# Where the first curve, three buffers, two low parts and one piece of weight work stand in a retention and two-layer MLP kernel on Trainium2

## The chip, the cores and the metric

The kernel runs on one core of one Trainium2 chip. The metric is the time of one execution on the device, in microseconds (us); lower is better. Five engines take part, each with its own queue that it works through strictly in order: TensorE (PE; PEld is its weight load), VectorE (DVE), ScalarE (ACT), GpSimd (POOL) and SyncE (SP), which issues the DMAs.

## What is computed

A retention layer (attention with a state that decays by a factor per head) gives 1536 tokens of 512 numbers. Two feed-forward layers follow, the first with softplus, the second with a scaled, shifted square of relu:

```python
def _moe_ref(x, w_in, w_out):
    h = x @ w_in                                        # 1536x512 @ 512x2048
    g = np.maximum(h, 0.0) + np.log1p(np.exp(-np.abs(h)))
    return (g @ w_out).astype(np.float32)

def _moe2_ref(x, w_in, w_out, s, b):
    h = x @ w_in
    r = np.maximum(h, 0.0)
    g = s * (r * r) + b
    return (g @ w_out).astype(np.float32)
```

The weights are 64-bit floats in memory.

## The kernel before

**Numbers in two parts.** Every operand of a matmul is a high part (`xh`, `wh`, `gh`: the value rounded by a ScalarE copy, L112) and a low part (`xl`, `wl`, `gl`: value less high part, by GpSimd, L115). A product is three matmuls: high by high, high by low, low by high. `split(hi, lo, src, hi_eng, lo_eng)` does both steps. A weight half is loaded as `raw` (pairs of words) and made into `wm` by three VectorE steps (L290, L292, L300) with a ScalarE step (L295) between them; then it is split.

**Tiles and pairs.** The tokens are three tiles j = 0, 1, 2 of 512. The 16 blocks of the 2048 hidden numbers are taken in pairs, p = 0 to 7 for each layer `la`. For tiles 0 and 1 a pair is computed by `second(la, p)` as a 2x2 matrix product with seven instead of eight products (sums of weight blocks `ws`, split to `sh`, `sl`; sums of inputs `x1` to `x4`). Each product is a `six`: six matmuls of 128x512. The four results are c11, c12, c22 and c21 (first index the half of the pair, second the tile). Tile 2 follows as two blocks of twelve (`all_of`).

**Banks.** The sixes go to three PSUM banks, `h` (the code's `one`), `y` (`other`) and `third`. A bank is copied out by ScalarE (`kept`, L514, to the buffers `p1`, `p5`, `u2`) or added to by VectorE (`joined`, L566), and only then is overwritten.

**The curve of layer one.** `begin` takes relu of the sum (ScalarE, L580) to r; `middle` forms u = -2r + sum, which is -|sum|, on VectorE (L592) and applies softplus on ScalarE (L593); `finish` adds r and u on GpSimd (L604) and puts the piece on the list `late_parts`; the next `end_part` takes it from there to `parts_g` (high part on ScalarE, low part on GpSimd). Where the sum still lies in a PSUM bank, L592 is the last that reads the bank. For c21 the sum is in bank `h`, and r and u go to named buffers (`tags`), before the change `u2` and `p1`.

**Second matmul.** `accs[k]` are twelve matmuls each (L630, or L403 for the blocks of the first stage) that multiply an earlier piece g by the second weights into four banks `acc`; each second such group is followed by the removal of `acc` into `xa` (additions on VectorE, L640; at the end of the first stage plain ScalarE copies, L410). The next group into `acc` waits for them.

**What sets the order.** The code is written in the order of issue for every engine; nothing is rearranged. `part`, `go_first`, `end_part` and `go_last` step generators that make the next weights: `go_first` issues two steps (L290, then L292 and L295), `end_part` the split of the weights before, `go_last` the third step.

**The place.** P0 = 2: `second(0, 2)` is the first pair computed this way, right after the retention stage and after `third_first`. It returns before tile 2, which `third_first` has done. There `accs` are: nothing, the last group of the first stage (with four L410 copies), and the two groups of tile 2. The pair after it, `second(0, 3)`, begins with a six into `h`, and its `accs[0]` and `accs[1]` use c11 and c21 of the pair before. The other touched place is `second(1, 2)` (`before`: the last pair before layer two also halves tile 2).

Of the kernel before, what the change touches and what calls it, by code (L numbers as in the profile page):

```python
# [41 lines left out]
P0 = FG // 2  # L42
# [6 lines left out]
def tile_retention_mlps(ctx: ExitStack, tc: tile.TileContext, head, w1, w2, sb, out):  # L49
    nc = tc.nc  # L50
# [560 lines left out]
    late_parts = []  # L611

    def parts_g(la, p, half, j, c):
        gg_t[la, p, half, j] = gh, gl = next_g()
        split(gh, gl, c, nc.scalar, nc.gpsimd)

    def acc_2(la, p, j, half, banks=FIRST + SECOND):
        wh, wl = w_t[la * NF + 2 * p + half, 1]
# [156 lines left out]
    with tc.manual_schedule():  # L775
# [135 lines left out]
        def part(to):  # L911

            nonlocal late_work, work
            late_work, work = work, split_next(to)
# [107 lines left out]
        def second(la, p, accs=None):  # L1022

            w = la * NF + 2 * p
            base = at[la, p + 1]
            halved = la and p >= HALVED
            final = not la and p == PAIRS - 1
            base -= halved
            (ah, al), (bh, bl), (sh, sl) = w_t[w, 0], w_t[w + 1, 0], s_t[w]
            a11, a12 = (ah[:, :KH], al[:, :KH]), (ah[:, KH:], al[:, KH:])  # L1030
            a22 = bh[:, KH:], bl[:, KH:]
            s1, s2, s3, s4 = ((sh[:, k], sl[:, k]) for k in range(4))
            b11, b21 = ((xh[0][:, k : k + 2], xl[0][:, k : k + 2]) for k in (0, 2))
            b22 = xh[1][:, 2:4], xl[1][:, 2:4]
            t1, t2, t3 = (x_t[k] for k in (1, 2, 3))

            of_tiles = (0, 1) if not la and p == P0 + 1 else (1, 2)
            accs = accs or [prior(la, p - 1, j, half) for j in of_tiles for half in range(2)]
            one, other, third = bank(ps_h, "h"), bank(ps_y, "y"), bank_2[1]

            before = la and p == HALVED - 1
            held = la and p == 1
            part(base + 2)
            six(one, a11, b11, True)
            p1 = kept(one, "p1")
            six(third, a12, b21, True)
            c11 = begin(la, joined(third, p1, not la), own=bool(la))
            end_part()
            go_first(bool(la))
            middle(c11)  # L1050
            accs[0]()
            if not held:
                finish(la, p, 0, 0, c11)
            go_last()
            if before:
                z = sum_z(3)
                next(z)

            part((base + 3) * (la or p != P0 + 1))
            six(other, s1, t1, True)  # L1060
            p5 = kept(other, "p5")
            six(one, s2, t2, False)
            u2 = kept(one, "u2")
            if held:
                finish(la, p, 0, 0, c11)
            end_part()
            go_first(bool(la))
            if before and not held:
                go(z, 2)
            accs[1]()  # L1070
            go_last()

            if final:
                part(base + 4)
                six(one, s3, t3, False)
                c22 = begin(la, joined(one, p5), own=True)
                end_part()
                go_first()
                middle(c22)
                accs[2]()  # L1080
                six(one, a22, x_t[4], False)
                c21 = begin(la, one, tags=("p5", "p1"))
                finish(la, p, 1, 1, c22)
                go_last()
                middle(c21)
                finish(la, p, 1, 0, c21)

                part(base + 5)
                six(other, s4, b22, False)
                c12 = begin(la, joined(other, u2, True))  # L1090
                end_part()
                go_first()
                middle(c12)
                accs[3]()
                finish(la, p, 0, 1, c12)
                go_last()
            else:
                part(base + 4)
                six(other, s4, b22, False)
                c12 = begin(la, joined(other, u2, not la), own=bool(la))  # L1100
                six(one, s3, t3, False)
                c22 = begin(la, joined(one, p5), own=True)
                if before:
                    if held:
                        go(z, 2)
                    else:
                        go(sum_z(1), 3)
                end_part()
                go_first(bool(la))
                middle(c12)  # L1110
                middle(c22)
                accs[2]()
                finish(la, p, 0, 1, c12)
                finish(la, p, 1, 1, c22)
                go_last()
                if before:
                    parts_z(3)

                part(base + 5)
                six(one, a22, x_t[4], False)  # L1120
                c21 = begin(la, one, tags=("u2", "p1"))
                if before and held:
                    go(sum_z(1), 3)
                end_part()
                go_first(bool(la))
                if not la and p == P0:
                    middle(c21)
                    accs[3]()
                else:
                    accs[3]()  # L1130
                    middle(c21)
                finish(la, p, 1, 0, c21)
                go_last()
                if before:
                    parts_z(1)

            if not la and p == P0:
                return
            if halved:
                last_tile(la, p, base, third, (a11, a12, a22), (s1, s2, s3, s4))  # L1140
                return
            part(base + 6)
            all_of(third, (ah, al), 2)
            ha = begin(la, third)
            end_part()
            go_first(bool(la))
            if before:
                go(sum_z(2), 2)
                go(sum_z(4), 2)
            middle(ha)  # L1150
            whole(*of_pair(la, p, 0, 0))
            finish(la, p, 0, 2, ha)
            go_last()
            if before:
                parts_z(2)
            if final:
                whole(*of_pair(la, p, 0, 1))
                x_whole(0)

            part(base + 7)  # L1160
            other = bank(ps_y, "y")
            all_of(other, (bh, bl), 2)
            hb = begin(la, other)
            end_part()
            go_first(bool(la))
            middle(hb)
            whole(*of_pair(la, p, *((1, 0) if final else (0, 1))))
            finish(la, p, 1, 2, hb)
            go_last()
            if final:  # L1170
                whole(*of_pair(la, p, 1, 1))
                x_whole(1)
                go(split_next(at[1, 1] + 1), 3)
            if before:
                parts_z(4)
# [171 lines left out]
```

## Time and profile before

| | us |
|---|---|
| median of 3 runs (563.3 to 563.73) | 563.42 |
| the profiled execution, its own time | 563.28 |
| its span, first to last instruction | 561.5 |
| TensorE busy in the span | 554.2 (99%) |
| VectorE / ScalarE / GpSimd busy | 388.4 / 362.6 / 384.4 |
| TensorE's waits that the profile names: 1.4 at the start, 1.2 on a copy L514, 0.9 on a low part L115, 0.2 on a high part L112 | 3.7 |

The span is what lies between the first and the last instruction; 1.8 us of the execution lie around it. A matmul's duration in the trace covers its way through the array, so neighbours overlap: in a dense row one starts every 0.227 us and lasts 0.39. The clock that was granted to TensorE was 1.00 of full speed over the whole span.

### The profile page before, as it was taken

The page shows a single profiled execution, that of the slowest core. Times are in us where ns is not written, and L with a number is a line of the kernel's source. Part 1 is how long each engine was busy: PE and PEld are TensorE (multiplying, and loading weights), DVE is VectorE, ACT ScalarE, POOL GpSimd, SP SyncE. Part 2 cuts the span into 40 slices and gives each one's busy share as a digit, 9 for nine tenths or more (in the row PEclk, how much of TensorE's full clock was granted, in tenths as well). Part 3 has the DMA queues.
Part 4 walks back from the last instruction along what each step waited for, and adds up shares of the span by engine and source line. Part 5 has one row for each costly group of instructions (what it writes and reads, how often), then busy time and mean ns, then how long its engine had stood idle before and what let it go on. Part 6 is the DMA issues. An engine that isn't in the chain of part 4 may idle for free.

```text
span 561.5 us, 8354 instructions
## 1 busy us (share of the span) xinstructions
PE 554.2 (99%) x3044; PEld 460.9 (82%) x3044; DVE 388.4 (69%) x588; ACT 362.6 (65%) x661; POOL 384.4 (68%) x323
## 2 busy tenths in 40 slices
PE   8999999999999999999999999999999999999997
PEld 7877888887688888888888887888788888888886
DVE  4887767776566958575789997598855655656334
ACT  4766662557456556555567888769497786868561
POOL 4457469879779796969797796749666655646230
PEclk9999999999999999999999999999999999999999
DMA  8996111211221312131231222221321121110005
GB/s 342 405 362 223 41 39 37 76 38 42 72 76 37 111 38 77 39 100 51 76 110 41 75 75 76 75 76 37 114 72 49 69 75 49 64 40 0 1 12 214
DMA packets 15017, 50.62 MB, mean 90 GB/s; under 512 B 1792, under 2 KB 2048, under 8 KB 14976
## 3 DMA queue, kind: packets, MB, share of 16 engines
q1 hardware_dynamic: 14976, 50.08, 25.6%
q8 instruction: 24, 0.39, 0.3%
q14 instruction: 17, 0.14, 0.1%
HBM read 46.93 MB, written 3.15 MB: 89 GB/s over the span
## 4 chain that ended last, share of the span: by engine, by line
PE 93%; DVE 3%; POOL 1%; ACT 1%; DMA 1%; issue 0%; POOLq 0%; DVEq 0%
PE acc L630 40%; PE h L500 12%; PE y L500 9%; PE acc L403 5%; PE h L352 5%; PE third L500 5%; PE y L508 4%; PE third L508 4%; PE y L191 2%; PE s L172 2%; PE h L191 1%; DVE p L551 1%; PE h L508 1%; PE y L352 1%; POOL gl L115 1%; PE acc L172 1%
## 5 line engine op out<-in xcount | busy, mean ns | idle before, releaser
L115 POOL TENSOR_TENSOR gl<-c,gh 128x512 fp32r<-128x512 f32 x78 | 103.2, 1331 | 65.0 <-ACT gh L112 45.3
L640 DVE TENSOR_TENSOR xa<-acc,xa 128x512 f32<-128x512 f32 x151 | 94.4, 683 | 76.0 <-PE acc L630 76.0
L115 POOL TENSOR_TENSOR wl<-wm,wh 128x512 fp32r<-128x512 f32 x64 | 86.7, 1355 | 77.9 <-ACT wh L112 77.8
L630 PE MATMUL acc<-wh,gh 128*128 128x512 f32 x190 | 74.3, 391 | 0.1
L630 PE MATMUL acc<-wh,gl 128*128 128x512 f32 x190 | 74.2, 391 | 0.0
L112 ACT ACTIVATE gh<-c 128x512 fp32r<-128x512 f32 x78 | 49.3, 631 | 13.1 <-POOL c L604 9.5
L630 PE MATMUL acc<-gl,wh 128*128 128x512 f32 x144 | 56.1, 390 | 0.9 <-POOL gl L115 0.9
L630 PE MATMUL acc<-gh,wh 128*128 128x512 f32 x144 | 56.3, 391 | 0.3 <-ACT gh L112 0.2
L630 PE MATMUL acc<-wl,gh 128*128 128x512 f32 x190 | 53.2, 389 | 0.0
L300 DVE SCALAR_TENSOR_TENSOR wm<-wm,cu,word 128x512 uint32<-128x512 uint32 x54 | 39.9, 739 | 4.2 <-ACT wm L295 3.5
L295 ACT ACTIVATE wm<-raw 128x512 f32<-128x512 f32 x64 | 42.4, 663 | 0.1
L292 DVE SCALAR_TENSOR_TENSOR word<-raw,cu,word 128x512 uint32<-128x512 uint32 x54 | 40.8, 756 | 1.9
L112 ACT ACTIVATE wh<-wm 128x512 fp32r<-128x512 f32 x64 | 39.7, 620 | 3.7 <-DVE wm L300 3.6
L630 PEld LDWEIGHTS acc<-wh,gh 128*128 128x128 f32 x190 | 35.8, 188 | 7.5 <-DVE xa L640 0.5
L630 PEld LDWEIGHTS acc<-wl,gh 128*128 128x128 f32 x190 | 35.7, 188 | 7.5
L630 PEld LDWEIGHTS acc<-wh,gl 128*128 128x128 f32 x190 | 35.8, 188 | 6.8
L599 ACT ACTIVATE c<-c,sbt 128x512 f32<-128x512 f32 x48 | 39.2, 816 | 1.6
L604 POOL TENSOR_TENSOR c<-c 128x512 f32<-128x512 f32 x28 | 36.8, 1323 | 4.3 <-ACT c L593 4.3
L630 PE MATMUL acc<-gh,wl 128*128 128x512 f32 x144 | 38.5, 389 | 0.0
L290 DVE TENSOR_SCALAR word<-raw 128x512 uint32<-128x512 uint32 x54 | 37.0, 686 | 0.5
L573 ACT ACTIVATE c<-c 128x512 f32<-128x512 f32 x21 | 13.1, 633 | 35.2 <-DVE c L566 35.2
L115 POOL TENSOR_TENSOR sl<-ws,sh 128x512 fp32r<-128x512 f32 x26 | 35.1, 1372 | 0.0
(277 smaller groups left out, 1406.7 us busy)
## 6 DMA issues: line engine op xcount, KB each, us to landing
raw<-w SPq DMA_DIRECT2D x64, 512.0 KB, 3.6
qk<-head SPq DMA_DIRECT2D x12, 512.0 KB, 8.3
kv<-head SPq DMA_DIRECT2D x12, 512.0 KB, 8.5
out<-xa SPq DMA_DIRECT2D x11, 256.0 KB, 2.1
cst<-head SPq DMA_DIRECT2D x1, 518.0 KB, 4.5
cst<-head SPq DMA_DIRECT2D x1, 256.0 KB, 5.5
out<-xa SPq DMA_DIRECT2D x2, 128.0 KB, 1.8
sbt<-sb SPq DMA_DIRECT2D x1, 1.0 KB, 10.3
```

The source lines that it names most:

```text
L112: nc.scalar.activation(hi, src, AF.Copy)
L115: lo_eng.tensor_tensor(out=lo, in0=src, in1=hi.bitcast(F32), op=ALU.subtract)
L290: nc.vector.tensor_scalar(out=x, in0=lw, scalar1=29, scalar2=None, op0=ALU.logical_shift_right)
L292: nc.vector.scalar_tensor_tensor(out=x, in0=hw, scalar=cu[:, 0:1], in1=x, op0=ALU.bitwise_and, op1=ALU.bitwise_or)
L295: nc.scalar.activation(m, hw.bitcast(F32), AF.Copy, scale=REBIAS)
L300: nc.vector.scalar_tensor_tensor(out=m.bitcast(U32), in0=m.bitcast(U32), scalar=cu[:, 1:2], in1=x, op0=ALU.logical_shift_left, op1=ALU.bit ...
L500: nc.tensor.matmul(ps, w[a][:, k * P : (k + 1) * P], x[b][:, k], start=start and i == 0, stop=i == len(ops) - 1, skip_group_check=True,)
L508: nc.tensor.matmul(ps, w[a][:, k * P : (k + 1) * P], (xh, xl)[b][j][:, k], start=i == 0, stop=i == len(ops) - 1)
L599: nc.scalar.activation(c, c, AF.Identity, scale=sbt[:, 0:1], bias=sbt[:, 1:2])
L604: nc.gpsimd.tensor_tensor(out=c, in0=c, in1=u, op=ALU.add)
L630: nc.tensor.matmul(acc_t[la, p, "pair", j][cc], *ops[i], start=half == 0 and i == 0, stop=half == 1 and i == 2)
L640: nc.vector.tensor_tensor(out=dst, in0=ps, in1=dst, op=ALU.add)
```

## The change

In `second(0, P0)`, named `first` below: the first curve (c11) is no longer begun right behind `joined`, but after the copies `p5` and `u2`; its `finish` and its high and low part come behind `accs[1]`. The curve of c21 uses the buffers `u2` and `p5`. The low parts of c12 and c22 go to VectorE. In `second(1, 2)` the step `go_first` of the last piece stands behind the group and its additions.

```diff
     def parts_g(la, p, half, j, c):
-        split(gh, gl, c, nc.scalar, nc.gpsimd)
+        split(gh, gl, c, nc.scalar, nc.vector if not la and p == P0 and j == 1 else nc.gpsimd)
...
+            first = not la and p == P0
...
-            c11 = begin(la, joined(third, p1, not la), own=bool(la))
+            c11 = joined(third, p1, not la)
+            if not first:
+                c11 = begin(la, c11, own=bool(la))
             end_part()
             go_first(bool(la))
-            middle(c11)
+            if not first:
+                middle(c11)
             accs[0]()
-            if not held:
+            if not (held or first):
                 finish(la, p, 0, 0, c11)
             go_last()
...
             u2 = kept(one, "u2")
+            if first:
+                c11 = begin(la, c11)
+                middle(c11)
...
             accs[1]()
+            if first:
+                finish(la, p, 0, 0, c11)
+                parts_g(*late_parts.pop())
             go_last()
...
-                c21 = begin(la, one, tags=("u2", "p1"))
+                c21 = begin(la, one, tags=("u2", "p5" if first else "p1"))
...
             end_part()
-            go_first(bool(la))
+            if not before:
+                go_first(bool(la))
             middle(hb)
             whole(*of_pair(la, p, *((1, 0) if final else (0, 1))))
+            if before:
+                go_first()
             finish(la, p, 1, 2, hb)
```

ScalarE's queue at the start of `second(0, 2)`: `c_1468` (after the change `c_1495`) is the relu of c11, L593 its softplus, `p5` and `u2` the copies, `wh0` high parts of weights, `gh` of c11, `xa2<-acc` the removal. Before:

```order
L514 ACTIVATE p1_1459<-h_1451 128x512
L580 ACTIVATE c_1468<-third_1171 128x512
L112 ACTIVATE wh0_1442<-wm_1444 128x512
L295 ACTIVATE wm_1475<-raw_1239 128x512
L593 ACTIVATE c_1470<-c_1470 128x512
L514 ACTIVATE p5_1491<-y_1452 128x512
L514 ACTIVATE u2_1499<-h_1451 128x512
L112 ACTIVATE gh_1501<-c_1468 128x512
L112 ACTIVATE wh0_1473<-wm_1475 128x512
L410 ACTIVATE xa2_111<-acc01_1332 128x512 x2
```

The same stretch of ScalarE's queue with the change:

```order
L514 ACTIVATE p1_1459<-h_1451 128x512
L112 ACTIVATE wh0_1442<-wm_1444 128x512
L295 ACTIVATE wm_1472<-raw_1239 128x512
L514 ACTIVATE p5_1485<-y_1452 128x512
L514 ACTIVATE u2_1493<-h_1451 128x512
L580 ACTIVATE c_1495<-third_1171 128x512
L593 ACTIVATE c_1497<-c_1497 128x512
L112 ACTIVATE wh0_1470<-wm_1472 128x512
L410 ACTIVATE xa2_111<-acc01_1332 128x512 x2
L410 ACTIVATE xa2_111<-acc2_1333 128x512
L410 ACTIVATE xa2_111<-acc3_1334 128x512
L112 ACTIVATE gh_1519<-c_1495 128x512
```

The two curve steps moved behind the two copies, the high part of c11 behind the removal, and the second weights' high part behind the softplus.

GpSimd's queue from the first weights' low part (`wl0`) to c22's sum (`c_1546`); the row `c_1468<-c_1468,c_1470` is c11's sum. Before:

```order
L115 TENSOR_TENSOR wl0_1443<-wm_1444,wh0_1442 128x512
L604 TENSOR_TENSOR c_1468<-c_1468,c_1470 128x512
L115 TENSOR_TENSOR gl_1502<-c_1468,gh_1501 128x512
L115 TENSOR_TENSOR wl0_1474<-wm_1475,wh0_1473 128x512
L319 TENSOR_TENSOR ws_1523<-wm_1475 128x256
L319 TENSOR_TENSOR ws_1523<-ws_1523,wm_1444 128x256
L319 TENSOR_TENSOR ws_1523<-wm_1444,wm_1475 128x256
L319 TENSOR_TENSOR ws_1523<-wm_1444,ws_1523 128x256
L604 TENSOR_TENSOR c_1535<-c_1535,c_1537 128x512
L604 TENSOR_TENSOR c_1546<-c_1546,c_1544 128x512
```

GpSimd's queue over the same work with the change:

```order
L115 TENSOR_TENSOR wl0_1443<-wm_1444,wh0_1442 128x512
L115 TENSOR_TENSOR wl0_1471<-wm_1472,wh0_1470 128x512
L604 TENSOR_TENSOR c_1495<-c_1495,c_1497 128x512
L115 TENSOR_TENSOR gl_1520<-c_1495,gh_1519 128x512
L319 TENSOR_TENSOR ws_1523<-wm_1472 128x256
L319 TENSOR_TENSOR ws_1523<-ws_1523,wm_1444 128x256
L319 TENSOR_TENSOR ws_1523<-wm_1444,wm_1472 128x256
L319 TENSOR_TENSOR ws_1523<-wm_1444,ws_1523 128x256
L604 TENSOR_TENSOR c_1535<-c_1535,c_1537 128x512
L604 TENSOR_TENSOR c_1546<-c_1546,c_1544 128x512
```

The second weights' low part now stands ahead of c11's sum and low part; the four sums of weights and the sums of c12 and c22 keep their places behind them.

VectorE's queue at the end of `second(0, 2)`, from the curves of c12 (`c_1537`) and c22 (`c_1544`) to that of c21, which reads bank `h_1451`. Before:

```order
L592 SCALAR_TENSOR_TENSOR c_1537<-c_1535,y_1452 128x512
L592 SCALAR_TENSOR_TENSOR c_1544<-c_1546,c_1544 128x512
L290 TENSOR_SCALAR word_1170<-raw_1287 128x512
L292 SCALAR_TENSOR_TENSOR word_1170<-raw_1287,cu_99,word_1170 128x512
L592 SCALAR_TENSOR_TENSOR p1_1582<-u2_1581,h_1451 128x512
L640 TENSOR_TENSOR xa2_111<-acc01_1552,xa2_111 128x512 x2
```

VectorE's queue there with the change:

```order
L592 SCALAR_TENSOR_TENSOR c_1537<-c_1535,y_1452 128x512
L592 SCALAR_TENSOR_TENSOR c_1544<-c_1546,c_1544 128x512
L115 TENSOR_TENSOR gl_1585<-c_1535,gh_1584 128x512
L115 TENSOR_TENSOR gl_1589<-c_1546,gh_1588 128x512
L290 TENSOR_SCALAR word_1170<-raw_1287 128x512
L292 SCALAR_TENSOR_TENSOR word_1170<-raw_1287,cu_99,word_1170 128x512
L592 SCALAR_TENSOR_TENSOR p5_1582<-u2_1581,h_1451 128x512
L640 TENSOR_TENSOR xa2_111<-acc01_1552,xa2_111 128x512 x2
```

The two low parts entered the queue ahead of the weight words and of the curve step of c21; on GpSimd they stood behind the two `sl`.

## Rows read from the trace of the kernel before

**Rows 1.** Waits of TensorE: who waited for whom, total, times, longest

```profile
PE y L500 <- ACT p L514: 1.2, 1, 1.2
```

**Rows 2.** TensorE in order of time, 125 to 151: start, us, what [idle before]

```profile
125.72 1.07 PE L403 MATMUL acc<-gh,wl 128*128 128x512 f32 x4
...
127.96 0.50 PE L500 MATMUL y<-xh,sh 128*128 128x512 f32 x1 [1.17 <-ACT p L514]
...
131.05 0.50 PE L630 MATMUL acc<-gh,wh 128*128 128x512 f32 x1
...
137.99 0.39 PE L500 MATMUL h<-xh,wh 128*128 128x512 f32 x1
...
146.85 0.50 PE L630 MATMUL acc<-gh,wh 128*128 128x512 f32 x1 [0.23 <-ACT gh L112]
148.27 0.50 PE L630 MATMUL acc<-gl,wh 128*128 128x512 f32 x1 [0.93 <-POOL gl L115]
...
150.90 0.39 PE L500 MATMUL y<-xh,sh 128*128 128x512 f32 x1
```

**Rows 3.** ScalarE in order of time, 124 to 139

```profile
126.79 0.63 ACT L593 ACTIVATE c<-c 128x512 f32<-128x512 f32 x1 [0.24 <-DVE c L592]
127.33 0.58 ACT L514 ACTIVATE p<-y 128x512 f32<-128x512 f32 x1
...
129.94 2.03 ACT L410 ACTIVATE xa<-acc 128x512 f32<-128x512 f32 x4
...
136.09 0.58 ACT L580 ACTIVATE u<-h 128x512 f32<-128x512 f32 x1
...
138.06 0.63 ACT L112 ACTIVATE gh<-c 128x512 fp32r<-128x512 f32 x1 [0.62 <-POOL c L604]
```

**Rows 4.** VectorE in order of time, 119 to 138

```profile
120.14 1.79 DVE L492 TENSOR_TENSOR x4l<-u,x4h 128x512 fp32r<-128x512 f32 x1
...
123.43 0.75 DVE L300 SCALAR_TENSOR_TENSOR wm<-wm,cu,word 128x512 uint32<-128x512 uint32 x1
...
134.13 0.68 DVE L290 TENSOR_SCALAR word<-raw 128x512 uint32<-128x512 uint32 x1
134.85 0.76 DVE L292 SCALAR_TENSOR_TENSOR word<-raw,cu,word 128x512 uint32<-128x512 uint32 x1
136.70 0.69 DVE L592 SCALAR_TENSOR_TENSOR p<-u,h 128x512 f32<-128x512 f32 x1 [1.10 <-ACT u L580]
```

**Rows 5.** GpSimd in order of time, 129 to 145

```profile
129.59 1.30 POOL L115 TENSOR_TENSOR gl<-c,gh 128x512 fp32r<-128x512 f32 x1 [0.74 <-ACT gh L112]
...
132.09 0.75 POOL L319 TENSOR_TENSOR ws<-wm 128x256 f32<-128x256 f32 x1
...
135.47 2.56 POOL L604 TENSOR_TENSOR c<-c 128x512 f32<-128x512 f32 x2
...
143.00 1.29 POOL L604 TENSOR_TENSOR u<-u,p 128x512 f32<-128x512 f32 x1
```

**Rows 6.** TensorE in order of time, 394 to 396 (layer two)

```profile
394.47 0.61 PE L500 MATMUL third<-xh,wl 128*128 128x512 f32 x2
395.14 0.50 PE L630 MATMUL acc<-wh,gh 128*128 128x512 f32 x1
```

**Rows 7.** VectorE in order of time, 392 to 397 (layer two)

```profile
392.42 0.68 DVE L290 TENSOR_SCALAR word<-raw 128x512 uint32<-128x512 uint32 x1
...
393.80 2.48 DVE L640 TENSOR_TENSOR xa<-acc,xa 128x512 f32<-128x512 f32 x4
```

**Rows 8.** Busy us by stretch: PE, PEld, DVE, ACT, POOL, granted clock, DMA share, GB/s

```profile
558.00:559.00 1.00, 0.47 (x4) 0.26 (x3) 0.64 (x2) 0.00 (x0) 0.00 (x0) 1.00 1.04 381
...
562.00:563.00 1.00, 0.00 (x0) 0.00 (x0) 0.00 (x0) 0.00 (x0) 0.00 (x0) 0.82 0.00 0
```

**Rows 9.** TensorE in order of time, 4 to 10: scores of one shape

```profile
4.48 1.23 PE L172 MATMUL s<-qk 64*128 64x128 f32 x8
...
8.88 0.71 PE L172 MATMUL s<-qk 64*128 64x128 f32 x8
```

More of the change, by code (lines that the diff above doesn't have):

```diff
@@ L1125, in second @@
                 go_first(bool(la))
-                if not la and p == P0:
+                if first:
                     middle(c21)
@@ L1135, in second @@
                     parts_z(1)
-            if not la and p == P0:
+            if first:
                 return
```

## The prediction

> **What bounds the kernel now.** I read the page's busy times first: TensorE works 99% of the span, so time can come or go only where TensorE waits, and every other engine counts only through that. Then the waits of TensorE: besides the start, the longest single one stands on a copy into `p5` [rows 1]. Then TensorE's order of time from 125 to 151 us, where that wait and the other two lie [rows 2]; a dense row there starts a matmul every 0.227 us (the last four of a group take 1.07, three steps and one duration of 0.39), and after a wait the next two starts lie about 0.13 further apart than that. Last the queues of ScalarE, VectorE and GpSimd over the same stretch [rows 3 to 5], since each piece of layer one passes through all three.
>
> Three gaps can be read. The group that starts its last four at 125.72 leaves TensorE free at 125.72 + 4 x 0.227 = 126.63, and the six into `y` starts at 127.96: 1.33 lost, because the copy of `y` (127.33 to 127.91) queued behind a softplus [rows 3]. From 137.99 to 150.90 stand 48 matmuls, 48 x 0.227 = 10.9 of 12.9 us: 2.0 lost, nearly all at 146.85 and 148.27, where TensorE waits for the high and the low part of c21, whose sum GpSimd only forms at 143.00 [rows 5]. In layer two, 394.47 + 2 x 0.227 = 394.92, and the next group starts at 395.14 [rows 6]: 0.22 and the slower start, 0.35.
>
> **Part one, the first curve behind the copies.** On ScalarE a pass follows another at about 0.52. The weights' `wm` is ready at 123.43 + 0.75 = 124.18 [rows 4], so without the curve ahead of them the queue runs: high part 124.2, L295 124.7, copy `p5` 125.3 to 125.9, copy `u2` 125.8, relu 126.2 to 126.8. TensorE finds the copy done and starts into `y` at 126.63, without a gap. Then VectorE's curve step 126.9 to 127.6, softplus 127.6 to 128.2, the second weights' high part 128.1, and the removal of the first stage's sums from 128.65 instead of 129.94. Its first two copies free the bank pair after half of 2.03 [rows 3], at 129.7. TensorE asks for that bank at 126.63 + 12 x 0.227 = 129.35 and waits 0.4, as it waited before. It starts at 129.75 instead of 131.05 [rows 2]. Gain so far 1.3; TensorE would then ask for bank `h` for the next pair at 129.75 + (137.99 - 131.05) = 136.7.
>
> **What that does to GpSimd.** The second weights' low part now stands ahead of c11's sum, and its high part comes from ScalarE only at 128.7. So: `wl` 128.8, sum of c11 130.05 to 131.35, high part on ScalarE 131.4 (behind the removal, which ends at 130.7), low part 132.1. Before, that low part ran at 129.59 and a weight part still followed it. From the first `ws` to the sums of c12 and c22 the queue took 135.47 - 132.09 = 3.4 [rows 5]. With 1.25 for the low part, `ws` now begins at 133.35 and the sums at 136.7, so that of c22 ends at 139.3, instead of 138.0. No work is added here; it comes 1.25 later.
>
> **Part two, two low parts on VectorE.** This is the term that decides. VectorE's queue is strict, and the two low parts now stand ahead of L290, L292 and c21's curve step L592, the last reader of bank `h`. Before, that step ran at 136.70, right behind its relu at 136.09 [rows 3, 4], and the next pair's six into `h` started at 137.99 without a wait. Now the second low part needs c22's high part: ScalarE 139.3 to 139.95 (before at 138.06). It starts at 140.0 at the earliest. How long it takes there is not shown: 0.69 is a VectorE pass alone, 1.79 one that subtracts two SBUF tiles while GpSimd works [rows 4], and here GpSimd works on (`sl`, right behind the sums). Behind it stand 0.68 + 0.76 + 0.69 = 2.1 [rows 4]. With 0.69 bank `h` comes free at 142.8; with 1.79 for both low parts (138.75, 140.55, 142.35) at 144.4. I take 143.9, since the row with 1.79 is the same operation on the same kinds of tiles. The Trainium skill, GPSIMD Engine Reference, section Specifications, says that GpSimd shares its SBUF interfaces with VectorE and contends with VectorE instructions that have two SBUF inputs; the 1.79 agrees, and by it the later end is the right one.
>
> So the next pair starts at 143.9 instead of 137.99: 5.9 later (4.8 to 6.4). TensorE stands idle from about 136.9 to 143.9, 7 us, where before it never waited over 1.4.
>
> **What the stall hides.** The three steps left of c21 (softplus 143.9, GpSimd's sum 144.6 to 145.9, then high and low part behind the next pair's copy and relu, about 150.2) are ready before TensorE asks for them, at 143.9 + 0.13 + 36 x 0.227 = 152.2. So the 2.0 of gaps after 137.99 go, but for the 0.13 of the restart: 1.9 back. GpSimd's relief of two passes and the free buffer `p1` (the next pair's copy no longer waits for the sum in `u2` and `p1`) would have been worth just that 1.9; they buy nothing more here. Net of the pair: 5.9 - 1.9 = +4.0 (2.9 to 4.5).
>
> **Part three, layer two.** The four additions L640 start at 393.80 behind L290 and L292, which began at 392.42 [rows 7]. Moved ahead, they start 1.4 earlier, the bank pair is free near 393.8, and TensorE goes on at 394.92: -0.35. The two weight steps end where the additions ended before, so L300 behind them, and with it the next weights, keep their time. ScalarE's L295 keeps its place in its own queue, and so does the load that SP issues with it.
>
> **The clock.** Before, TensorE's granted clock stayed at the upper of its two levels, 2.4 GHz, with no wait over 1.4 us. It falls once, behind the end: its last matmuls lie in the second 558 to 559 (0.47 us of it busy), and the second 562 to 563 has a mean of 0.82, so it fell to the lower level, 1.2 GHz, about 4 us after the last matmul [rows 8]. An idle time of 7 us is longer than that, so I expect it to fall in the stall. At the lower level half of the time is lost. For how long, no row shows directly; nearest is the kernel's start, where eight score matmuls took 1.23 at 4.48 and the same eight 0.71 at 8.88 [rows 9], although the page notes the full clock for both. TensorE began there at 1.45, so slow work lasted between 4.3 and 7.4 us, worth 2.1 to 3.7. I take 2.3, near the lower end, as matmuls stand denser behind the stall. The bound below is 0. The Trainium skill, TensorE: Matmul & The Clock Gate, section "HAM oscillation — how this bites in real kernels", says that a TensorE that waits long between two bursts of matmuls begins the next burst at the lower clock; it speaks against this change, and the one fall in the trace agrees.
>
> **The sum**, against the profiled execution's 563.28 (0.14 below the median of 563.42, which I leave aside): +4.0 for the pair, -0.35 for layer two, +2.3 for the clock, about +5.9: 569.2.
>
> **The rivals.**
> - *The stall without the clock.* TensorE's stall is shorter than 7, or the clock falls late or not at all: 563.28 + 4.0 - 0.35 = 566.9, with the bounds of the stall 565.8 to 567.5. For it speaks that nothing in the kernel shows a wait between 1.4 and 4 us; against it the fall behind the end. 0.25.
> - *The change does what its places suggest, and nothing is held.* This asks that c22's high part is there before c21's relu, so that VectorE's two low parts fit into its idle time before 136.70. Then the gaps go: 1.3 + 1.9 + 0.35 = 3.6 less, 559.7. It decides at the end of c22's sum on GpSimd: it must come by about 135, and even before it ended at 138.0 behind the same sums [rows 5]. 0.04.
> - *The hold is small.* If GpSimd gets to the sums some 3 us earlier than I work out, the stall is about 3 us and cancels with the gains: 562.2 to 564.4 (within 0.2%). It would take the weights' low part off the wait for ScalarE, and the queue rows show no such way. 0.04.
> - *A larger loss*, from a clock that stays down longer, 571 and more. 0.07.
>
> **How the numbers follow.** Forecast 0.60 (568.2 to 570.8). The range runs from 566.0, which takes in most of the case without the clock, to 571.0; outside it lie the faster and the even case, the lowest part of the first rival and the larger loss, about 0.2. Faster by over 0.2% (1.1 us, about what a measurement of this kernel can tell from no change) 0.04, within it 0.04, slower 0.92.
>
> **What would show it.** Right: in the new trace the six into `y` near 126.6 without a wait; TensorE idle for some 6 to 7 us ahead of the six into `h` of the next pair, released by L592 on VectorE, and ahead of that two L115 on VectorE, the second waiting for ScalarE's `gh`; no wait at the group that uses c21; a granted clock below 1.00 right behind the stall and matmuls twice as far apart there; no gap at the group in layer two. Wrong: L592 of c21 within a microsecond of its relu, or a six into `h` that starts ahead of it. If the stall is there and the clock stays at 1.00, the first rival holds and only the 2.3 falls.

## The result, and the profile after the change

The changed kernel takes 569.15 us (median of 4 runs, 568.42 to 569.39), the kernel before 563.44 on the same chip (4 runs, 563.30 to 563.73). The ratio is 1.0098, 95% interval 1.0081 to 1.0116: slower by 5.7 us, about 1%. The profiled execution of after took 568.42, with a span of 566.6 and a mean granted clock of 0.997; the rows below come from it. It is the fastest of the four runs: one of the others had the same mean clock (568.98), two had 0.994 (569.32 and 569.39).

The page's busy times of after (us, share of the span, instructions):

```profile
PE 555.2 (98%) x3044; PEld 462.4 (82%) x3044; DVE 390.6 (69%) x590; ACT 363.0 (64%) x661; POOL 382.9 (68%) x321
```

The waits of TensorE in the touched pair, after (who waited for whom, total, times, longest):

```profile
PE h L500 <- DVE p L592: 5.0, 1, 5.0
PE h L500 <- DVE c L566: 1.4, 1, 1.4
PE acc L630 <- ACT xa L410: 0.3, 1, 0.3
```

The shares of busy time hardly moved. What moved is in the waits: the one on the copy into `p5` [rows 1] is gone and so are those of c21's group [rows 2]; a wait of 5.0 us on L592 and one of 1.4 on L566 have come. TensorE in order of time, after (start, us, what, idle time before and who ended it):

```profile
126.90 0.39 PE L500 MATMUL y<-xh,sh 128*128 128x512 f32 x1
...
130.12 0.50 PE L630 MATMUL acc<-gh,wh 128*128 128x512 f32 x1 [0.34 <-ACT xa L410]
...
134.50 0.50 PE L500 MATMUL h<-x4h,wh 128*128 128x512 f32 x1 [1.37 <-DVE c L566]
...
143.88 0.79 PE L500 MATMUL h<-xh,wh 128*128 128x512 f32 x1 [5.00 <-DVE p L592]
144.47 0.63 PE L500 MATMUL h<-xl,wh 128*128 128x512 f32 x1
...
148.17 0.40 PE L630 MATMUL acc<-gh,wh 128*128 128x512 f32 x1
...
153.63 0.39 PE L630 MATMUL acc<-gh,wh 128*128 128x512 f32 x1
...
156.35 0.39 PE L500 MATMUL y<-xh,sh 128*128 128x512 f32 x1
```

Read against [rows 2]: the six into `y` starts without a wait, the next pair's six into `h` at 143.88 instead of 137.99, c21's group (153.63) without a wait, and the next six into `y` at 156.35 instead of 150.90, 5.45 later. Of that 0.27 was there before the pair began: its first six into `h` starts at 118.74 here and at 118.47 before, in code that the change doesn't touch.

Why bank `h` came so late is read from the chain of waits of after over this stretch (start, us, what ran):

```profile
137.09 2.53 POOL c L604 x2
...
139.65 0.64 ACT gh L112
...
140.31 1.53 DVE gl L115
141.84 0.62 DVE word L290
...
142.48 0.76 DVE word L292
143.23 0.60 DVE p L592
...
143.88 2.50 PE h L500 x5
```

From the bottom up: the six into `h` waits for L592, which only stands in VectorE's queue behind the two weight words and the second low part; that one waits for ScalarE's high part of c22, and this for GpSimd's sums. L592's own input, c21's relu, had been there since 138.28, as ScalarE in order of time shows:

```profile
137.70 0.58 ACT L580 ACTIVATE u<-h 128x512 f32<-128x512 f32 x1
```

VectorE in order of time, after:

```profile
133.76 0.69 DVE L566 TENSOR_TENSOR c<-h,p 128x512 f32<-128x512 f32 x1 [4.60 <-POOL gl L115]
...
139.07 2.76 DVE L115 TENSOR_TENSOR gl<-c,gh 128x512 fp32r<-128x512 f32 x2 [3.24 <-ACT gh L112]
```

The engine that took over the low parts because it had room stood idle for 3.24 us right before them.

The granted clock, microsecond by microsecond (stretch, its length, busy us of TensorE, its weight load, VectorE, ScalarE and GpSimd, granted clock, DMA share, GB/s):

```profile
142.00:143.00 1.00, 0.00 (x0) 0.00 (x0) 0.96 (x2) 0.00 (x0) 0.97 (x1) 1.00 0.00 0
143.00:144.00 1.00, 0.12 (x1) 0.13 (x1) 1.00 (x3) 0.15 (x1) 0.00 (x0) 0.79 0.00 0
144.00:145.00 1.00, 1.00 (x3) 0.81 (x4) 1.00 (x3) 0.48 (x1) 0.44 (x1) 0.50 0.69 209
...
146.00:147.00 1.00, 1.00 (x3) 0.73 (x3) 0.87 (x2) 0.16 (x1) 0.00 (x0) 0.51 0.01 4
147.00:148.00 1.00, 1.00 (x6) 0.81 (x5) 0.00 (x0) 0.44 (x1) 0.00 (x0) 1.00 0.00 0
```

It fell from 2.4 to 1.2 GHz at the end of the stall, some 0.3 us before TensorE began again at 143.88 (a mean of 0.79 from 143 to 144), and rose again at 147.0. The twelve matmuls from 143.88 to 148.17 took 4.29; at full speed with a restart's 0.13 they take 12 x 0.227 + 0.13 = 2.85, so the clock cost 1.44 in this execution. The Trainium skill, TensorE: Matmul & The Clock Gate, section "HAM oscillation — how this bites in real kernels", says that matmuls behind a long wait start at the lower clock; the 0.50 from 144 on agrees.

In layer two the gap is gone: TensorE's group starts 0.45 behind the last two into `third` (two steps of 0.227), where [rows 6] has 0.67. TensorE in order of time, after:

```profile
399.96 0.62 PE L500 MATMUL third<-xh,wl 128*128 128x512 f32 x2
400.41 0.39 PE L630 MATMUL acc<-wh,gh 128*128 128x512 f32 x1
```

VectorE in order of time, after, with the additions now ahead of L290, where [rows 7] has them behind it:

```profile
397.91 2.47 DVE L640 TENSOR_TENSOR xa<-acc,xa 128x512 f32<-128x512 f32 x4
400.31 0.68 DVE L290 TENSOR_SCALAR word<-raw 128x512 uint32<-128x512 uint32 x1
```

The account of the profiled executions: 0.27 from ahead of the pair, 5.45 - 0.27 - 1.44 = 3.74 for the pair, 1.44 for the clock, about -0.35 in layer two: 5.10 of the 568.42 - 563.28 = 5.14.

### The profile page after: what moved, and what is told of

It is laid out like the page before. It is cut to its first block, busy times and chain, and to the rows that moved or that the text cites. A ratio compares the mean times of both kernels' runs of the same rounds, so it can differ in the third digit from the quotient of the medians.

```text
span 566.6 us, 8352 instructions
## 1 busy us (share of the span) xinstructions
PE 555.2 (98%) x3044; PEld 462.4 (82%) x3044; DVE 390.6 (69%) x590; ACT 363.0 (64%) x661; POOL 382.9 (68%) x321
## 4 chain that ended last, share of the span: by engine, by line
PE 95%; DVE 2%; POOL 1%; ACT 1%; issue 0%; DVEq 0%
PE acc L630 39%; PE h L500 12%; PE y L500 9%; PE acc L403 6%; PE third L500 5%; PE h L352 5%; PE y L508 5%; PE third L508 5%; PE y L191 2%; PE s L172 2%; PE h L191 1%; PE h L508 1%; PE y L352 1%; PE acc L796 1%; POOL c L604 1%; PE acc L172 1%
## 5 line engine op out<-in xcount | busy, mean ns | idle before, releaser
L640 DVE TENSOR_TENSOR xa<-acc,xa 128x512 f32<-128x512 f32 x151 | 94.3, 683 | 77.1 <-PE acc L630 77.0
L115 POOL TENSOR_TENSOR gl<-c,gh 128x512 fp32r<-128x512 f32 x76 | 100.8, 1333 | 65.1 <-ACT gh L112 47.8
L290 DVE TENSOR_SCALAR word<-raw 128x512 uint32<-128x512 uint32 x54 | 37.0, 686 | 0.5
```

What stands on the lines that cost most here:

```text
L115: lo_eng.tensor_tensor(out=lo, in0=src, in1=hi.bitcast(F32), op=ALU.subtract)
L290: nc.vector.tensor_scalar(out=x, in0=lw, scalar1=29, scalar2=None, op0=ALU.logical_shift_right)
L640: nc.vector.tensor_tensor(out=dst, in0=ps, in1=dst, op=ALU.add)
```

## Experiments

The theory: VectorE's strict queue holds c21's curve step L592, and with it bank `h`, behind two low parts that wait for GpSimd's and ScalarE's work; TensorE stalls, and the stall costs the clock as well. The rivals: the new order of GpSimd's queue (c11's sum later) makes the loss; or VectorE and GpSimd slow each other; or the loss is the clock's alone. Two parts of the change could be gains that the stall covers. The ratio is to the kernel before in runs on the same chip; it is worked out over all runs and need not be the quotient of two medians.

| kernel | median us | ratio, 95% |
|---|---|---|
| after, low parts back on GpSimd | 562.45 | 0.9985 [0.9976, 0.9994] |
| before, low parts on VectorE | 567.29 | 1.0074 [1.0061, 1.0086] |
| before, first curve moved | 564.81 | 1.0026 [1.0016, 1.0036] |
| before, layer two's piece | 563.00 | 0.9991 [0.9983, 1.0000] |
| before, buffers and layer two's piece | 561.21 | 0.9967 [0.9955, 0.9979] |
| after, matmuls in the stall | 566.75 | 1.0055 [1.0043, 1.0067] |
| after, c22 in its own buffer | 569.23 | 1.0097 [1.0085, 1.0109] |
| after, c21's curve ahead | 567.72 | 1.0084 [1.0064, 1.0105] |
| the same, low parts behind the additions | 562.91 | 0.9989 [0.9980, 0.9997] |
| the gains together | 560.10 | 0.9936 [0.9924, 0.9948] |

### The low parts back on GpSimd

The changed kernel, with one line undone:

```diff
-        split(gh, gl, c, nc.scalar, nc.vector if not la and p == P0 and j == 1 else nc.gpsimd)
+        split(gh, gl, c, nc.scalar, nc.gpsimd)
```

> The changed kernel with the two low parts of c12 and c22 back on GpSimd; all else of the change stays. Theory (VectorE's queue held by the two low parts makes the loss): the curve step L592 of c21 runs within 1 us of its relu, the next pair's six into bank h waits under 0.5 us instead of 5.0, no fall of the clock; the low part of c21 is then late on GpSimd (near 147.9 in the changed kernel's times); time 562.4 us (562.0 to 563.0), 6.7 below the changed kernel. Rival (GpSimd's new order, the second weights' low part ahead of c11's sum, makes the loss, since the sums come 1.6 later): the wait into bank h stays at 3 us or more and the time stays above 565.

562.45 (11 runs, 562.21 to 563.44), against 563.38 before: 6.7 less than after, and faster than before. VectorE in order of time:

```profile
138.12 0.69 DVE L592 SCALAR_TENSOR_TENSOR p<-u,h 128x512 f32<-128x512 f32 x1 [1.09 <-ACT u L580]
```

TensorE in order of time, the six into `h`:

```profile
138.87 0.50 PE L500 MATMUL h<-xh,wh 128*128 128x512 f32 x1 [0.17 <-DVE p L592]
```

L592 runs right behind its relu, and the stall of 5.0 is a wait of 0.17. GpSimd's order is the changed one here, so the rival that blames it falls: with the rest of the change in place, the whole loss hangs on which engine makes two low parts.

### The low parts alone on VectorE

The kernel before, with that one line of the change.

> The kernel before with nothing changed but the two low parts of c12 and c22 on VectorE. Theory (the hold): GpSimd's order is that of before, so c22's high part comes at 138.1 to 138.7 as before, the second low part ends near 139.9 and L592 near 141.9; the six into bank h starts near 142.0 instead of 137.99, the 2.0 of waits for c21 go: +2.1 without a fall of the clock, +3.5 with one as in the changed kernel; 565.5 to 567.0 us. Rival (GpSimd's new order makes the loss): no wait into bank h, gain from the relieved GpSimd, 562 us or less.

567.29, 0.3 above the top of the range that I had expected. TensorE in order of time:

```profile
142.31 0.50 PE L500 MATMUL h<-xh,wh 128*128 128x512 f32 x1 [4.11 <-DVE p L592]
```

The windows of the same kernel (columns as above):

```profile
140.00:142.00 2.00, 0.00 (x0) 0.00 (x0) 1.96 (x4) 0.00 (x0) 1.40 (x1) 1.00 0.00 0
142.00:143.00 1.00, 0.69 (x2) 0.58 (x3) 1.00 (x3) 0.63 (x1) 0.00 (x1) 0.85 0.20 49
143.00:144.00 1.00, 1.00 (x4) 0.78 (x3) 1.00 (x3) 0.00 (x0) 1.00 (x1) 0.50 0.90 340
144.00:146.00 2.00, 2.00 (x6) 1.52 (x5) 1.30 (x3) 0.60 (x1) 0.28 (x1) 0.50 0.17 68
```

The line alone makes the stall: 4.11 of waiting, the six 142.31 - 137.99 = 4.3 later. The clock fell here too, and only when TensorE had already begun again. 4.3 less the 1.9 of hidden waits leaves 2.4 of the 3.9 that were lost, so some 1.5 for the clock.

### The first curve alone

The kernel before, with the parts of the diff for the first curve (begin, middle, finish and parts of c11 behind the copies and `accs[1]`).

> The kernel before with only the first curve of the pair behind the copies and its low part behind the first group (buffers u2 and p1, low parts on GpSimd, layer two as before). Theory: the wait on the copy p5 (1.33) goes, but c22's sum waits for c11's low part (as in the changed kernel, 1.4 at the fourth six into h) and GpSimd's sums come 1.6 later, so c21's low part comes near 148.7: 0.5 later than before; no stall over 1.5 us; 563.9 us (563.4 to 564.4). Rival (GpSimd's new order makes the loss): a wait of 3 us or more into bank h, 566 us or more. Had the front gained what its own wait is worth: 562.1.

564.81, 1.4 slower than before, where I had expected 0.5: above the range. There is no long stall. ScalarE in order of time:

```profile
145.69 0.60 ACT L514 ACTIVATE p<-h 128x512 f32<-128x512 f32 x1 [4.54 <-POOL u L604]
```

TensorE in order of time:

```profile
149.64 0.50 PE L630 MATMUL acc<-gl,wh 128*128 128x512 f32 x1 [0.92 <-POOL gl L115]
```

The next pair's copy waits for c21's sum, which still reads `p1`, and c21's high and low part stand behind that copy. GpSimd forms that sum at 144.38 instead of 143.00 [rows 5]. So its later order shifts the whole chain: c21's low part is used at 149.64 instead of 148.27 [rows 2], 1.37 later, which is the loss. The 1.3 that the front gains at the six into `y` is lost again on the way, at the fourth six into `h`, which waits 1.36 for L566. Alone this part of the change is a loss.

### Layer two alone, and with the buffers

The kernel before with layer two's piece, and with that and c21's buffers (of the two names only one differs from before, `p5` in place of `p1`):

```diff
-            go_first(bool(la))
+            if not before:
+                go_first(bool(la))
             middle(hb)
             whole(*of_pair(la, p, *((1, 0) if final else (0, 1))))
+            if before:
+                go_first()
```

```diff
-                c21 = begin(la, one, tags=("u2", "p1"))
+                c21 = begin(la, one, tags=("u2", "p1" if la or p != P0 else "p5"))
```

> The kernel before with only the weight piece in layer two behind the additions. Theory: the four L640 start 1.4 earlier, TensorE's gap of 0.22 and its slower start there go, nothing else moves: 0.35 less, 563.05 us (562.9 to 563.3). Rival (the next weights come later by the two steps, and a wait grows elsewhere): 563.4 or more.

> The kernel before with only c21's buffers u2 and p5 and the moved weight piece in layer two. Theory: the next pair's copy p1 no longer waits for c21's sum, so that c21's high part runs right behind the sum (144.3) and its low part ends at 146.3, when TensorE asks for it: the waits at 146.85 and 148.27 and before the six at 144.97 go, 1.9 us; layer two 0.35; 561.2 us (560.9 to 561.8). Rival (the waits for c21 come from GpSimd's load, two low parts ahead of the sum, not from the buffer): they stay, and only 0.35 is gained: 563.1.

563.00 against 563.42, and 561.21 against 563.38. Layer two's piece is worth 0.42 by the medians; the interval ends at 1.0000, so the time alone hardly tells it from nothing, but its trace shows the gap of [rows 6] gone. TensorE in order of time, with layer two's piece:

```profile
394.52 0.62 PE L500 MATMUL third<-xh,wl 128*128 128x512 f32 x2
394.97 0.39 PE L630 MATMUL acc<-wh,gh 128*128 128x512 f32 x1
```

The buffers are worth 563.00 - 561.21 = 1.8. With the buffers no wait at c21's group is left, and of the pair's waits the one on the copy remains, as in [rows 1]. TensorE in order of time, with the buffers:

```profile
128.16 0.50 PE L500 MATMUL y<-xh,sh 128*128 128x512 f32 x1 [1.16 <-ACT p L514]
```

So the free buffer alone takes away both waits at 146.85 and 148.27; it needs neither the low parts on VectorE nor the moved curve.

### Matmuls in the stall

The changed kernel, with twenty matmuls into bank `third` ahead of the next pair's first six. They add nothing to the output, since the next product overwrites that bank.

```diff
             part(base + 2)
+            if not la and p == P0 + 1:
+                for _ in range(20):
+                    nc.tensor.matmul(third, a11[0][:, :P], b11[0][:, 0], start=True, stop=True)
             six(one, a11, b11, True)
```

> The changed kernel with 20 extra matmuls of 128x512 into the free bank third, put in TensorE's queue right ahead of the next pair's first six into bank h, so inside the stall; their result is overwritten and changes nothing in the output. Theory (the six into h waits for VectorE's L592, and the stall costs more than its length because the clock falls in it): the extra work of 20 x 0.227 = 4.5 us fits into the wait of 5.0, the six still starts when L592 ends, the granted clock stays 1.00, and the 1.4 us of half-speed matmuls behind the stall go: 567.6 us (567.2 to 568.0), 1.2 to 2 below the changed kernel. Rival (the stall alone makes the loss and the clock has no part): no change, 569.2. Rival (TensorE itself is short of time there): 4.5 us longer.

566.75, 2.4 below after (569.15). Its mean granted clock is 1.000 in every run. TensorE in order of time:

```profile
138.55 4.70 PE L1047 MATMUL third<-xh,wh 128*128 128x512 f32 x20
143.74 0.50 PE L500 MATMUL h<-xh,wh 128*128 128x512 f32 x1 [0.49 <-DVE p L592]
```

Bank `h` comes free at nearly the same time as in after (the six start at 143.74, there at 143.88), and useless work in the stall makes the kernel faster. So the clock is a part of the loss, and the 566.75 - 563.48 = 3.3 that stay are the pair's 3.7 less layer two's 0.4. How large the clock's part is differs between runs: the two profiled executions lie 568.42 - 566.83 = 1.6 apart, which the 1.44 of after's trace and the 0.14 of the earlier start make up; the medians lie 2.4 apart, and the runs of after that make the difference have no trace.

### c22 in a buffer of its own

After's rows show one wait that I had not foreseen: c22's sum L566 waits 4.60 for GpSimd, since its result goes to the buffer in which c11's relu stays until c11's low part is made. The changed kernel, with that sum in the buffer `p1`:

```diff
-                c22 = begin(la, joined(one, p5), own=True)
+                c22 = begin(la, joined(one, p5, to=late.tile([P, TT], F32, tag="p1", name="c22") if first else None), own=True)
```

> The changed kernel with c22's sum in the buffer p1, which is free there, instead of the buffer that c11's relu still occupies. This takes away the wait of 1.4 us at the fourth six into h (on VectorE's L566, which waits for GpSimd's low part of c11), which the prediction had not seen. Theory (the end of the stall is set by ScalarE's high part of c22 and VectorE's two low parts): TensorE reaches the stall 1.4 earlier and waits 6.4 there instead of 5.0; L592 ends as before; time unchanged, 569.2 us (568.5 to 569.6). Rival (the missed wait is a part of the loss): 1.4 less, 567.8.

569.23, the same as after. TensorE in order of time:

```profile
143.66 0.79 PE L500 MATMUL h<-xh,wh 128*128 128x512 f32 x1 [6.63 <-DVE p L592]
```

The windows (columns as above):

```profile
137.00:140.00 3.00, 0.04 (x1) 0.00 (x0) 1.07 (x1) 2.30 (x5) 3.00 (x3) 0.87 0.00 0
140.00:144.00 4.00, 0.34 (x1) 0.34 (x2) 3.88 (x5) 0.98 (x3) 2.75 (x2) 0.50 0.00 0
...
148.00:150.00 2.00, 2.00 (x7) 1.52 (x6) 0.74 (x2) 0.01 (x1) 0.00 (x0) 0.64 0.00 0
```

The wait of 1.37 is gone and the stall is 1.6 longer; its end stays. The clock fell earlier in the stall and came back later, within the last of these windows. So the end of the stall does not hang on when TensorE arrives, but on the chain GpSimd, ScalarE, VectorE.

### c21's curve ahead of the low parts

The changed kernel, with c21's curve step L592 ahead of the two low parts, which stay on VectorE:

```diff
+                if first:
+                    middle(c21)
                 end_part()
                 go_first(bool(la))
                 if first:
-                    middle(c21)
                     accs[3]()
```

> The changed kernel with the two low parts still on VectorE, but c21's curve step L592 (and its softplus) ahead of them in the queues. Theory (only the place of the two low parts in VectorE's queue makes the loss, not that VectorE does them): the six into h waits under 0.5 us, c21's low part comes ahead of TensorE's need because GpSimd is relieved, no fall of the clock; 562.0 us (561.6 to 562.6), 0.4 below the kernel with the low parts back on GpSimd (562.45). Rival (two low parts on VectorE cost by themselves, through the SBUF interface shared with GpSimd): above 563.

567.72, where I had expected 562.0: a clear miss. TensorE in order of time:

```profile
138.83 0.50 PE L500 MATMUL h<-xh,wh 128*128 128x512 f32 x1 [0.18 <-DVE p L592]
...
145.63 0.47 PE L630 MATMUL acc<-gh,wh 128*128 128x512 f32 x1 [3.77 <-DVE xa L640]
```

VectorE in order of time:

```profile
140.00 2.90 DVE L115 TENSOR_TENSOR gl<-c,gh 128x512 fp32r<-128x512 f32 x2 [1.22 <-ACT gh L112]
...
144.20 2.48 DVE L640 TENSOR_TENSOR xa<-acc,xa 128x512 f32<-128x512 f32 x4
```

The windows (columns as above):

```profile
144.00:146.00 2.00, 0.37 (x2) 0.36 (x3) 2.00 (x5) 0.00 (x0) 0.03 (x1) 1.00 0.26 76
146.00:148.00 2.00, 2.00 (x7) 1.53 (x6) 2.00 (x5) 0.02 (x1) 0.00 (x0) 0.53 0.49 186
```

The stall at `h` is gone, as expected, and a stall of 3.77 stands at the next group, with a fall of the clock behind it: behind the same two low parts wait the weight words and the four additions L640, which free the banks `acc`. I had followed the one held instruction and not the rest of the queue.

### The low parts behind the additions as well

The kernel just above, with the two low parts also behind the four L640, still on VectorE (its L1147 is the low part):

```diff
+                    for *k, c in late_parts:
+                        gh, gl = gg_t[tuple(k)] = next_g()
+                        nc.scalar.activation(gh, c, AF.Copy)
+                        lows.append((gl, c, gh))
...
                     accs[3]()
+                    for gl, c, gh in lows:
+                        nc.vector.tensor_tensor(out=gl, in0=c, in1=gh.bitcast(F32), op=ALU.subtract)
```

> As the kernel with c21's curve step ahead, with the two low parts still on VectorE, but behind the four removals L640 as well. There the stall had moved to those removals (3.8 us), which stood behind the two low parts. Theory (whatever stands behind the two low parts in VectorE's queue waits for ScalarE's high parts, and TensorE stalls on the first of it that it needs): neither the six into h nor the group into acc waits over 0.5; the next in the queue is the next pair's joined L566, which comes near 146 instead of 142, so c21's high part comes near 147 and its low part near 149, a wait of about 1.5 at that group; no fall of the clock; 563.8 us (563.3 to 564.4). Rival (VectorE's two low parts slow everything by the shared SBUF interface): a stall of 3 us or more stays, 566 or more.

562.91, 0.9 better than I had expected and below the range, and 6.2 below after with the same work on the same engines. VectorE in order of time:

```profile
142.36 1.84 DVE L1147 TENSOR_TENSOR gl<-c,gh 128x512 fp32r<-128x512 f32 x2
```

TensorE in order of time, the longest wait behind that place:

```profile
148.03 0.50 PE L630 MATMUL acc<-gl,wh 128*128 128x512 f32 x1 [0.62 <-POOL gl L115]
```

The two low parts now find their input there and take 0.96 each instead of 1.31 (both are means of the groups by form), with GpSimd idle from 143.04 on. There is no stall over 1.4 and the clock is 1.000. So it is the place in the queue: VectorE's added work does not make the loss, and its contention with GpSimd only a small part of it. The Trainium skill, GPSIMD Engine Reference, section Specifications, names contention of GpSimd with VectorE instructions that read two SBUF tiles; the 1.31 beside GpSimd and the 0.96 with little beside it agree. For the two low parts together that is at most some 0.7 us, of a stall of 5.

### The gains together

The kernel before, with the first curve moved, c21 in `u2` and `p5` and layer two's piece as in the change; the low parts stay on GpSimd, c11's sum stands ahead of the second weights' low part, c22's sum goes to `p1`, and c21's curve, sum and parts stand ahead of the split of the weight sums and of c12's and c22's parts. The core of it, against the kernel before:

```diff
+                c11 = begin(la, c11)
+                middle(c11)
+                finish(la, p, 0, 0, c11)
+                later = late_parts.pop()
...
+                if first:
+                    middle(c21)
+                    finish(la, p, 1, 0, c21)
+                    go(late_work, 1)
+                    later = [late_parts.pop(), *late_parts]
+                    late_parts.clear()
                 end_part()
```

> A kernel that is meant to beat both: the changed kernel with the low parts on GpSimd; c11's sum ahead of the second weights' low part; c22's sum in buffer p1; c21's relu, curve step, softplus and sum ahead of the split of the weight sums; c21's high and low part ahead of those of c12 and c22. Theory: bank h is free before TensorE asks for it, c21's low part is there in time, so the front's 1.2 and the 1.9 at c21 are both kept, and 0.35 in layer two: 559.9 us (559.6 to 560.6). Rival (GpSimd is the bound of this stretch, so that one gain eats the other): 561.2 or more, like the kernel with only the buffers and the piece in layer two.

560.10 (559.85 to 560.28), 3.4 faster than before: the best of all. Of TensorE's waits (who waited for whom, total, times, longest) one is left in the pair:

```profile
PE acc L630 <- ACT xa L410: 0.3, 1, 0.3
```

The three gains that the prediction found (1.3 at the six into `y`, 1.9 at c21's group, 0.35 in layer two, 3.6 in all) are there to be had, 3.4 of them here, by an order that holds no bank.

## Why the prediction was right

**The front**, 1.3 gained: exact. Less the 0.27 by which this execution was late before the pair began, the six into `y` starts at 126.63, as worked out, and the group into `acc` at 129.85 (129.75 foreseen, with a wait of 0.34 for 0.4).

**GpSimd's sums 1.25 later**: the sum of c22 ends at 139.6; 139.3 was foreseen, and 0.27 of the difference is that delay.

**The missed step.** "TensorE would then ask for bank `h` for the next pair at 136.7" failed. The prediction moved c11's low part behind the removal but did not follow the buffer that this keeps: the addition L566 that forms c22 waits for it, bank `h` is handed on late one six earlier, and TensorE loses 1.37 at 134.50. So it asked for bank `h` at 138.7 (137.81 + 4 x 0.227) and the stall was 5.0, not the 6 to 7 that I gave as a mark. The forecast didn't suffer, because the end of the stall was worked out from the chain and not from where it began; the run with c22 in a buffer of its own shows that.

**The hold by two low parts**, bank `h` at 143.9: the six started at 143.88. That it fits so closely is luck. My 143.9 is 140.0 + 1.79 + 2.1: it gives the longer of the two durations to the second low part alone, since with both at 1.79 the sum was 144.4. In the trace the first low part took 1.09 and ended before the second had its input; the second took 1.53 (140.31 to 141.84), 0.26 less than my 1.79, and the 0.27 that this execution was late before the pair began, which was not in the sum, made up for it. The hold is 143.88 - 0.27 - 137.99 = 5.6, for 5.9.

**What the stall hides**, 1.9: c21's group ran without a wait, and the pair's net is 3.74 for 4.0, so 5.62 - 3.74 = 1.9.

**Layer two**, -0.35: 0.22 and the slower start are gone in the trace; -0.42 by the medians.

**The clock**, 2.3: 1.44 in the profiled execution, 2.4 by the medians of after and of the kernel with matmuls in the stall. The rival without the clock, 566.9, is what that kernel measured: 566.75. So the term is right in kind, and that its size fits the medians is luck: 2.3 is a slow stretch of 4.6 us, taken from the kernel's start, where the page notes the full clock, and the profiled run has 3.4 us from 143.6 to 147.0. What differs in the runs with a mean clock of 0.994 has no trace for after; as an estimate, that mean over a span of 567.4 is 2 x 0.006 x 567.4 = 6.8 us at the lower level. In the run with c22's own buffer, whose profiled mean is 0.991, the clock fell earlier and stayed down until 149.4.

**The rivals** on the other side fell by their own condition: c22's sum on GpSimd ended at 139.6, not by 135.

**What the prediction had not seen** is the price of the front alone: it counted 1.3 as gained there and called c21's waits hidden by the stall. Without the stall the later sums cost 1.4 through the copy into `p1`, as the run with the first curve alone shows. And its list of what stands behind the low parts ended at L592; the miss with the curve ahead showed that the four additions L640 behind it are as dear.

## What to carry to other kernels

Before an operation goes to an engine with idle time, write down what stands behind it in that engine's queue and who waits for each, to the last one: an operation whose input comes late holds all of them, and an instruction that frees a bank or a buffer for TensorE must stand ahead of it. Work out a stall's end from the chain that releases it, not from when the waiting engine arrives, and add what the clock loses behind it. And where one change holds several parts, cost each as if it were alone: here a free buffer was worth 1.8 us, and the move of two low parts to an engine with room cost 569.15 - 562.45 = 6.7 beside the other parts and 567.29 - 563.38 = 3.9 alone.

## What the runs showed of the hardware

- The clock falls in waits that I would have taken for short: with 4.11 us of waiting in the kernel before with VectorE's low parts it fell (0.85 from 142 to 143), and there only when TensorE had begun again; with 3.77 us in the kernel with c21's curve ahead likewise (1.00 until 146, 0.53 from 146 to 148). With a wait of 6.63 it was 0.50 for all of 140 to 144, where TensorE stood until 143.66, its last matmul having ended near 137.0; at the kernel's end before the change it fell some 4 us after the last matmul [rows 8].
- Twenty useless matmuls in a stall of 5 us made the kernel 2.4 us faster by the medians.
- With the stall idle, the mean clock differed between runs of one kernel: 0.997 in two of after's four runs (568.42 and 568.98) and 0.994 in two (569.32 and 569.39). With matmuls in the stall it was 1.000 in all five (566.68 to 566.84).
- A subtraction of two tiles on VectorE took 1.31 us beside GpSimd's own and 0.96 with GpSimd mostly idle; GpSimd's pair of `sl` took 3.40 in after and 2.57 before.
